# A 64-column copy moved from ScalarE to GpSimd in a fused attention and FFN kernel, with the order of all instructions planned anew

## The chip, the cores and the metric

The kernel runs on one core of one Trainium2 chip. The metric is the device time of one execution in microseconds (us), the median of several runs. The engines are TensorE (PE: matmul; PEld: its weight load), VectorE (DVE), ScalarE (ACT), GpSimd (POOL) and SyncE (SP), which here issues every DMA.

## The reference

What is computed, cut to what matters (8 batches, 8 heads, 576 positions, head size 64; 4608 tokens of width 512, FFN width 2048; all float32):

```python
scores = scale * np.matmul(q, k.transpose(0, 1, 3, 2))
thresh = np.max(scores, axis=-1, keepdims=True) - tau
scores = np.where(scores >= thresh, scores, -1000000000.0)
scores = scores - np.max(scores, axis=-1, keepdims=True)
attn = np.exp(scores)
attn = attn / (np.sum(attn, axis=-1, keepdims=True) + 1e-09)
x = np.matmul(attn, v)          # heads side by side: 4608 x 512
...
h = x @ w_in
r = np.maximum(h, 0.0)
return (s * (r * r) + b) @ w_out
```

## The kernel before, in words

**Pieces.** Float32 products are made of float16 pieces: a number is scaled, its high piece is its float16 value, its low piece the float16 value of the rest, and a product of two numbers is high x high + high x low + low x high. The helper `product` (line 327) writes the two 64-column halves of such a matmul side by side, so nearly all matmuls have line 327. Only batch 0 is computed in float32 (`plain_tile`, 36 tiles, at the start, while the weights are loaded and split).

**Tiles of attention.** Batches 1 to 7 are 252 split tiles (`split_tile`, line 621), each 128 queries of one head (or the last 64 of two heads) by 576 keys. A tile runs through all engines:

- TensorE makes the scores in bank s or t (line 643, 641).
- VectorE takes the row's maximum (line 646). GpSimd makes the threshold out of it (line 648, one column), ScalarE the bias (line 650) and the exponentials (line 652).
- VectorE drops what is below the threshold and sums the row (line 654). GpSimd adds the small constant (line 657, one column), VectorE takes the reciprocal (line 659).
- ScalarE writes the high pieces, `pieces[:, 0:S]` with S = 576 (line 660). Line 662 copies their first T = 64 columns to the columns S to S + T; ScalarE does it. VectorE writes the low pieces to the columns from S + T on (line 663).
- SyncE transposes `pieces[:, T:2S + T]`, that is high pieces 64 to 575, the copied 64, then the low pieces, into ea or eb (line 668). It waits for lines 660, 662 and 663. The buffer `en` is one of three.
- When a pair of heads has its tiles, TensorE multiplies ea and eb by the values (`with_v`, line 678), and ScalarE takes the result out of bank pv (line 685).

**The FFN.** When a block of 256 tokens is there, it runs in 16 steps of 128 FFN columns: TensorE makes h (24 matmuls), ScalarE takes the relu out of PSUM (line 902), squares it (905) and rounds it to the high piece (906), GpSimd makes the low piece (line 907, 128x256; VectorE in the last block), and TensorE multiplies by the second weights into bank o. Attention tiles of the next batches run among the steps of the earlier blocks.

**What sets the order.** The order of all instructions on each engine is made by a planner (`Plan`) before the kernel is emitted. Each operation is added with an engine, two costs in ns (how long it occupies the engine, and when its result is there), what it reads and writes, and a due time in tiles. `act`, `pool`, `dve` and `dve2` (lines 366 to 376) add for one engine; `dve2` and `pool` mark the operation as a user of one shared port, of which the planner lets only one run at a time. The planner places the operations by their due times forwards and backwards, then corrects single due times by the list `NUDGES` (from line 26), and places once more:

```python
for kind, n, many, by in NUDGES:
    for k in kinds[kind][n:n + many]:
        first[k] += by
```

A kind is all operations with the same engine and first cost, numbered as they first appear; an entry moves the due time of `many` of them, from the n-th on, by `by` ns. Kind 56 is the copy of line 662, 252 operations. Kinds 62 and 67 are TensorE's first and second products of the FFN, kind 45 small loads, kind 58 the transposes. Each engine runs its instructions strictly in the planned order; waits are on semaphores of the others.

Of the kernel before, what the change touches and what calls it, by code (L numbers as in the profile page):

```python
# [243 lines left out]
def tile_attention_ffn(ctx: ExitStack, tc: tile.TileContext, qT, kT, v, tau, w_in, w_out, s, b, out):  # L244


    nc = tc.nc
    P = 128
    B, H, D, S = qT.shape
# [3 lines left out]
    T = S - M  # L253
# [118 lines left out]
    def act(cost, fn, r, w, at):  # L372
        plan.add("ACT", cost, fn, r, w, at)
# [800 lines left out]
```

## Time and profile before

| | |
|---|---|
| runs | 1104.88, 1105.57, 1108.40 us; median 1105.57 us |
| the profiled execution | 1103.84 us, of which the span (first to last instruction) is 1102.0 us |
| granted TensorE clock | 1.00 of full speed (2.4 GHz), in the mean and in every slice |
| instructions | 38579 |
| DMA | 157.05 MB moved, mean 143 GB/s |

The profile was taken of one execution. Its rows give, for an engine or a group of instructions, the busy time, the mean of one, and the idle time of the engine just ahead of it with what ended that idle time (its releaser). The spans of matmuls have modelled ends, and spans on GpSimd are rough. Idle time of an engine that is not the bottleneck costs nothing by itself.

### The profile page before, as it was taken

The page shows a single profiled execution, that of the slowest core. Times are in us where ns is not written, and L with a number is a line of the kernel's source. Part 1 is how long each engine was busy: PE and PEld are TensorE (multiplying, and loading weights), DVE is VectorE, ACT ScalarE, POOL GpSimd, SP SyncE. Part 2 cuts the span into 40 slices and gives each one's busy share as a digit, 9 for nine tenths or more (in the row PEclk, how much of TensorE's full clock was granted, in tenths as well). Part 3 has the DMA queues.
Part 4 walks back from the last instruction along what each step waited for, and adds up shares of the span by engine and source line. Part 5 has one row for each costly group of instructions (what it writes and reads, how often), then busy time and mean ns, then how long its engine had stood idle before and what let it go on. Part 6 is the DMA issues. An engine that isn't in the chain of part 4 may idle for free.

```text
span 1102.0 us, 38579 instructions
## 1 busy us (share of the span) xinstructions
PE 1085.7 (99%) x15122; PEld 934.5 (85%) x15122; DVE 916.0 (83%) x1948; ACT 964.3 (88%) x2293; POOL 543.9 (49%) x1115
## 2 busy tenths in 40 slices
PE   8999999999999999999999999999999999999998
PEld 7767778899888888988888889988888888888888
DVE  6899999999999899989898999979989887984022
ACT  7998989999999989998989898989989998996443
POOL 6546555555545555545554455535445554542300
PEclk9999999999999999999999999999999999999999
DMA  9940269789988899888787888879797776583000
GB/s 275 362 160 2 68 151 197 125 168 183 189 140 157 143 199 152 166 132 172 161 136 124 155 165 162 139 118 185 153 176 122 156 134 142 95 126 61 7 21 21
DMA packets 359222, 157.05 MB, mean 143 GB/s; under 512 B 313344, under 2 KB 340736, under 8 KB 359040
## 3 DMA queue, kind: packets, MB, share of 16 engines
q1 hardware_dynamic: 359040, 154.60, 71.3%
q8 instruction: 118, 1.93, 0.8%
q14 instruction: 64, 0.52, 0.2%
HBM read 46.01 MB, written 9.44 MB: 50 GB/s over the span
## 4 chain that ended last, share of the span: by engine, by line
PE 69%; ACT 12%; DVE 8%; DMA 6%; issue 4%; SPq 1%; POOL 1%; ACTq 0%; DVEq 0%; POOLq 0%
PE o L327 24%; PE h L327 23%; PE pv L678 7%; PE s L327 5%; PE t L327 5%; DMA eb<-en 3%; ACT en L660 3%; ACT em L652 2%; DMA ea<-en 2%; DVE em L654 2%; ACT iw L902 1%; DVE en L663 1%; DVE st L646 1%; PE t L601 1%; PE pv L614 1%
## 5 line engine op out<-in xcount | busy, mean ns | idle before, releaser
L327 PEld LDWEIGHTS <-iw 128*64 128x64 f16 x6912 | 392.9, 110 | 28.6 <-issue 5.7
L327 PE MATMUL h<-xp,iw 128*64 128x256 f16 x6456 | 406.4, 273 | 2.2 <-ACT iw L902 1.6
L327 PEld LDWEIGHTS <-gs 128*64 128x64 f16 x3552 | 242.0, 110 | 74.4 <-issue 0.2
L907 POOL TENSOR_TENSOR gs<-iw,gs 128x256 f16<-128x256 f32 x272 | 197.6, 727 | 191.9 <-ACT gs L906 77.7
L327 PE MATMUL o<-ow,gs 128*64 128x512 f16 x1890 | 242.6, 379 | 0.0
L663 DVE SCALAR_TENSOR_TENSOR en<-em,st,en 128x576 f16<-128x576 f32 x252 | 208.7, 831 | 23.6 <-ACT en L660 21.6
L660 ACT ACTIVATE en<-em,st 128x576 f16<-128x576 f32 x252 | 193.5, 770 | 14.8 <-DVE st L659 6.0
L327 PE MATMUL o<-iw,gs 128*64 128x512 f16 x1470 | 191.6, 379 | 0.0
L648 POOL TENSOR_SCALAR st<-st,wz 128x1 f32<-128x1 f32 x252 | 125.3, 498 | 109.9 <-DVE st L646 75.8
L657 POOL TENSOR_SCALAR st<-st 128x1 f32<-128x1 f32 x252 | 89.5, 355 | 135.9 <-DVE em L654 87.2
L902 ACT ACTIVATE iw<-h 128x256 f32<-128x256 f32 x269 | 101.6, 378 | 43.8 <-PE h L327 38.0
L905 ACT ACTIVATE iw<-iw 128x256 f32<-128x256 f32 x288 | 119.5, 416 | 3.4
L906 ACT CAST gs<-iw 128x256 f16<-128x256 f32 x288 | 115.6, 403 | 4.9 <-PE o L327 0.7
L327 PEld LDWEIGHTS <-ow 128*64 128x64 f16 x1568 | 101.6, 110 | 13.3 <-issue 0.5
L654 DVE SCALAR_TENSOR_TENSOR em<-t,st,em 128x576 f32<-128x576 f32 x126 | 102.2, 811 | 12.3 <-ACT em L652 6.3
L654 DVE SCALAR_TENSOR_TENSOR em<-s,st,em 128x576 f32<-128x576 f32 x126 | 102.1, 810 | 8.4 <-ACT em L652 5.5
L652 ACT ACTIVATE em<-t,st,wz 128x576 f32<-128x576 f32 x126 | 104.1, 827 | 2.3 <-DVE en L663 1.4
L652 ACT ACTIVATE em<-s,st,wz 128x576 f32<-128x576 f32 x126 | 104.1, 826 | 1.0
L646 DVE TENSOR_REDUCE st<-s 128x1 f32<-128x576 f32 x126 | 94.5, 750 | 11.7 <-PE s L327 10.8
L646 DVE TENSOR_REDUCE st<-t 128x1 f32<-128x576 f32 x126 | 94.5, 750 | 9.7 <-PE t L327 8.7
L650 ACT ACTIVATE st<-st,wz 128x1 f32<-128x1 f32 x252 | 73.1, 290 | 19.5 <-DVE st L646 18.6
L678 PE MATMUL pv<-eb,ow 128*64 128x256 f16 (+1 forms) x588 | 78.9, 286 | 0.9 <-DMA eb<-en 0.9
(198 smaller groups left out, 1649.8 us busy)
## 6 DMA issues: line engine op xcount, KB each, us to landing
ow<-k SPq DMA_DIRECT2D x98, 216.0 KB, 3.9
rk<-in_k_dram SPq DMA_DIRECT2D x29, 288.0 KB, 3.8
iw<-in_moe_w_in_dram SPq DMA_DIRECT2D x16, 512.0 KB, 9.5
ow<-in_moe_w_out_dram SPq DMA_DIRECT2D x16, 512.0 KB, 9.6
rq<-in_q_dram SPq DMA_DIRECT2D x28, 288.0 KB, 3.8
out_dram<-iw SPq DMA_DIRECT2D x31, 256.0 KB, 3.0
rv<-in_v_dram SPq DMA_DIRECT2D x56, 128.0 KB, 3.2
qs<-k SPq DMA_DIRECT2D x14, 216.0 KB, 3.4
```

The source lines that it names most:

```text
L327: nc.tensor.matmul(out[own], stat[:, own], moving, start=start, stop=stop)
L646: dve((667, 750), lambda: nc.vector.tensor_reduce(out=top, in_=ps, axis=mybir.AxisListType.XY, op=ALU.max, negate=True), [bk], [(ks_, 0)], ...
L648: pool((290, 255), lambda: nc.gpsimd.tensor_scalar(out=line, in0=top, scalar1=-1.0, scalar2=va.wz[:, 2:3], op0=ALU.mult, op1=ALU.add), [(k ...
L652: act((716, 885), lambda: nc.scalar.activation(out=halves, in_=ps, func=AF.Exp, bias=bias, scale=va.wz[:, 1:2]), [bk, (ks_, 4), (va.kwz, 1 ...
L654: dve((738, 820), lambda: nc.vector.scalar_tensor_tensor(out=halves, in0=ps, scalar=line, in1=halves, op0=ALU.is_ge, op1=ALU.mult, accum_o ...
L660: act((666, 760), lambda: nc.scalar.activation(out=pieces[:, 0:S], in_=ex, func=AF.Copy, scale=unit), [em_k, (ks_, 3)], [en_k], i)
L663: dve2((728, 830), lambda: nc.vector.scalar_tensor_tensor(out=pieces[:, S + T:2 * S + T], in0=ex, scalar=unit, in1=pieces[:, 0:S], op0=ALU ...
L678: nc.tensor.matmul(ps[j * D:(j + 1) * D], hd.values()[:, (n + 1) % 5, u * D:(u + 1) * D], lazy[("ea", "eb")[j]][:, n, g.c0:g.c0 + g.n], st ...
L902: act((264, 400), lambda: nc.scalar.activation(out=g(), in_=ps, func=AF.Relu, scale=H_DOWN), [h, (f"w{SPARES[(0, 1, 5)[k3]]}", "i", 2)], [ ...
L905: act((307, 430), lambda: nc.scalar.activation(out=g(), in_=g(), func=AF.Square), [kg], [kg], at)
L906: act((295, 405), lambda: nc.scalar.copy(out=hi, in_=g()), [kg], [f"gh{k3}"], at)
L907: do((735, 735) if not self.last else (400, 490), lambda: eng.tensor_tensor(out=lo, in0=g(), in1=hi, op=ALU.subtract), [kg, f"gh{k3}"], [f ...
```

## The change

Line 662 becomes an instruction of GpSimd, with other costs for the planner (occupied 260 ns, result after 250 ns, where ScalarE had 135 and 225), and with GpSimd's mark as a user of the shared port. It reads and writes the same columns and has the same place in the program; what waits for it is the same. In `NUDGES` the 34 entries of kind 56, which belonged to the old copy, are taken out; 321 entries are appended, over 57 kinds, among them 7 for kind 56, which is now GpSimd's copy, 39 for kind 67, 22 for kind 45, 20 for kind 62 and 17 for kind 58. The list goes from 655 entries to 942. Nothing else is changed. The diff, with most of the list cut:

```diff
 NUDGES = (
...
-    (73, 2, 6, -4809), (23, 7, 17, -916), (62, 5, 5, 3875), (25, 17, 19, -13768), (49, 34, 22, 1138), (29, 2, 2, -2426), (56, 148, 6, -6574), (74, 6, 2, -4235),
+    (73, 2, 6, -4809), (23, 7, 17, -916), (62, 5, 5, 3875), (25, 17, 19, -13768), (49, 34, 22, 1138), (29, 2, 2, -2426), (74, 6, 2, -4235), (21, 166, 10, 12067),
...
+    (67, 514, 46, 349), (22, 208, 1, 2624), (62, 52, 3, -1385), (53, 243, 9, 901), (43, 3, 3, 8544), (11, 7, 4, 907), (38, 44, 5, 5396), (13, 31, 1, 4746),
+    (69, 13, 2, -1317), (72, 3, 3, -2323), (45, 69, 5, -924), (55, 196, 4, 7572), (50, 78, 15, -6298), (68, 11, 1, -949),
 )
...
         act((666, 760), lambda: nc.scalar.activation(out=pieces[:, 0:S], in_=ex, func=AF.Copy, scale=unit),
             [em_k, (ks_, 3)], [en_k], i)
-        act((135, 225), lambda: nc.scalar.copy(out=pieces[:, S:S + T], in_=pieces[:, 0:T]), [en_k], [(en_k, 1)], i)
+        pool((260, 250), lambda: nc.gpsimd.tensor_copy(out=pieces[:, S:S + T], in_=pieces[:, 0:T]), [en_k], [(en_k, 1)], i)
         dve2((728, 830), lambda: nc.vector.scalar_tensor_tensor(
             out=pieces[:, S + T:2 * S + T], in0=ex, scalar=unit, in1=pieces[:, 0:S], op0=ALU.mult, op1=ALU.subtract),
             [em_k, en_k, (ks_, 3)], [(en_k, 2)], i)
```

## Rows read from the trace of the kernel before

**Rows 1.** The page, busy time, share and instructions of each engine.

```profile
PE 1085.7 (99%) x15122; PEld 934.5 (85%) x15122; DVE 916.0 (83%) x1948; ACT 964.3 (88%) x2293; POOL 543.9 (49%) x1115
```

**Rows 2.** Windows: stretch, length, then busy us (instructions) of each engine, clock, DMA.

```profile
100.00:200.00 100.00, 99.43 (x1377) 79.03 (x1373) 92.75 (x182) 93.22 (x214) 54.49 (x95) 1.00 0.60 124
200.00:300.00 100.00, 99.06 (x1436) 88.34 (x1433) 95.63 (x209) 95.50 (x239) 56.72 (x115) 1.00 0.89 167
300.00:400.00 100.00, 98.99 (x1437) 85.85 (x1434) 90.83 (x199) 92.54 (x228) 53.64 (x109) 1.00 0.87 155
400.00:500.00 100.00, 98.75 (x1442) 88.59 (x1438) 92.72 (x197) 92.83 (x232) 48.90 (x104) 1.00 0.91 159
500.00:600.00 100.00, 99.45 (x1431) 86.23 (x1427) 88.28 (x192) 89.65 (x218) 53.47 (x108) 1.00 0.78 151
600.00:700.00 100.00, 98.46 (x1434) 89.04 (x1431) 91.56 (x189) 90.31 (x222) 50.72 (x102) 1.00 0.82 157
700.00:800.00 100.00, 99.70 (x1439) 86.61 (x1436) 89.08 (x188) 91.19 (x225) 48.23 (x105) 1.00 0.82 147
800.00:900.00 100.00, 99.90 (x1445) 86.71 (x1441) 88.01 (x186) 93.24 (x224) 51.67 (x104) 1.00 0.79 145
900.00:1000.00 100.00, 100.00 (x1454) 86.98 (x1452) 83.10 (x178) 91.35 (x227) 48.08 (x102) 1.00 0.71 125
sum 900.00, PE 893.73 PEld 777.38 DVE 811.97 ACT 829.84 POOL 465.93; mean PE 99.30 PEld 86.38 DVE 90.22 ACT 92.20 POOL 51.77
```

**Rows 3.** Waits of TensorE from 100 us on: us in total, times, longest.

```profile
PE pv L678 <- DMA eb<-en: 2.2, 3, 1.3
PE h L327 <- ACT iw L902: 1.6, 6, 0.4
PE pv L327 <- ACT x L685: 0.6, 2, 0.4
PE s L327 <- DVE em L654: 0.5, 1, 0.5
PE pv L327 <- ACT xt L685: 0.5, 1, 0.5
```

**Rows 4.** Timeline, TensorE, at 581.94 us: start, us, engine, instruction, idle before.

```profile
581.94 1.28 PE L327 MATMUL h<-xp,iw 128*64 128x256 f16 x20 [0.44 <-ACT iw L902]
```

**Rows 5.** Groups of instructions by line: busy us, mean ns, then idle before.

```profile
L662 ACT COPY en<-en 128x64 f16<-128x64 f16 x252 | 59.3, 238 | 0.9
L663 DVE SCALAR_TENSOR_TENSOR en<-em,st,en 128x576 f16<-128x576 f32 x252 | 208.7, 831 | 23.6 <-ACT en L660 21.6
L648 POOL TENSOR_SCALAR st<-st,wz 128x1 f32<-128x1 f32 x252 | 125.3, 498 | 109.9 <-DVE st L646 75.8 <-DVE st L659 19.3 <-ACT gs L906 3.0
L657 POOL TENSOR_SCALAR st<-st 128x1 f32<-128x1 f32 x252 | 89.5, 355 | 135.9 <-DVE em L654 87.2 <-DVE st L659 13.1 <-ACT iw L902 5.0
L451 POOL TENSOR_SCALAR qs<-qs,bound 128x576 f32<-128x576 f32 x2 | 1.5, 743 | 2.2 <-ACT em L585 2.2
```

**Rows 6.** Single lines: ns min/median/max, first and last start; landing of line 668's transposes.

```profile
L657 POOL TENSOR_SCALAR st<-st x252: 192/192/1158, 136.9 to 995.0; 128x1 f32<-128x1 f32 x126
...
L648 POOL TENSOR_SCALAR st<-st,wz x252: 257/268/1464, 130.5 to 991.1; 128x1 f32<-128x1 f32 x126
...
L663 DVE SCALAR_TENSOR_TENSOR en<-em,st,en x252: 792/814/1307, 144.5 to 998.0; 128x576 f16<-128x576 f32 x126
...
DMA to landing us min/median/max: 2.8/3.7/6.7
```

**Rows 7.** Timeline, VectorE and GpSimd, 600.60 to 601.46 us, inside one tile.

```profile
600.60 0.82 DVE L663 SCALAR_TENSOR_TENSOR en<-em,st,en 128x576 f16<-128x576 f32 x1
...
600.77 0.69 POOL L657 TENSOR_SCALAR st<-st 128x1 f32<-128x1 f32 x1 [0.92 <-ACT iw L902]
```

**Rows 8.** Waits of SyncE's queue: us in total, times, longest.

```profile
SPq L668 <- DVE en L663: 144.0, 101, 5.5
...
SPq L668 <- ACT en L662: 44.7, 32, 2.6
```

188 rows, old and new, of the table NUDGES are left out of this document.

## The prediction

> **What bounds the kernel now.** First the busy table: TensorE is busy 1085.7 of 1102.0 us, ScalarE 964.3, VectorE 916.0, GpSimd 543.9 [rows 1]. Only 16.3 us of the span have no matmul in them, so the kernel is bound by TensorE, and its matmuls are not touched. The change can give back no more than the time that TensorE waits. Where is that time? The stretches of 100 us show it [rows 2]: from 100 to 1000 us TensorE is busy 893.73 of 900 us, idle 6.27; the low pieces of all 252 split tiles run between 144 and 999 us [rows 6], so the change works inside this stretch. The other 10.1 us (16.3 less 6.27) lie before 100 us, where loads and plain tiles set the pace, and at the very end, where the last output block leaves.
>
> A busy TensorE is not one at its peak, because ends of matmuls are modelled, so I look for hidden waits in the same rows by counting matmuls: 1454 in the stretch from 900 to 1000 us, which has no idle time, against 1431 to 1445 in the seven others from 200 on. Summing 1454 less each count over the seven stretches from 200 to 900 us gives 18+17+12+23+20+15+9 = 114 matmuls, and at 14.54 matmuls per us that is 7.8 us. The mix of sizes differs a little and some records may be missing, so 7.8 us is an estimate. It and the 6.27 us say the same: six to eight microseconds is what the split stage could give back.
>
> Who ends these waits? In TensorE's list of waits from 100 us on [rows 3], 2.7 us of the 5.4 us shown end with ScalarE (1.6 after the relu of the FFN's first product, 0.6 and 0.5 after evacuations of the values), 2.2 us with transposes that land in eb, 0.5 us with VectorE. So half of TensorE's waits are on ScalarE, which is busy 92.2% of that stage; VectorE is next with 90.2%, GpSimd has 51.8% [rows 2]. One such wait stands in the timeline at 581.94 us: the matmuls of h wait 0.44 us for a relu [rows 4].
>
> **The change, part by part.**
>
> The copy leaves ScalarE: 252 instructions of 238 ns on average, 59.3 us in all, go [rows 5]. ScalarE's share in the split stage falls from 829.84 of 900 us to about 770.5, 85.6%. That is not time off the span. It shortens ScalarE's queue by 0.24 us in each tile, and the relu or evacuation behind it comes that much earlier.
>
> The copy comes to GpSimd: no copy of 128x64 f16 is in the trace. From below, a one-column operation (line 657) takes 192 ns at least [rows 6]; from above, a 576-column one of f32 (line 451) takes 743 ns [rows 5]. On the line between them 64 columns cost 192 + 63/575 x 551 = 252 ns. I take 0.25 us because 64 columns are much nearer to one.
>
> It does not run beside VectorE's low pieces in the good sense. The timeline shows it [rows 7]: the low pieces (line 663) run from 600.60 to 601.42 us, and a one-column operation of GpSimd that began at 600.77 took 0.69 us instead of 0.19, ending at 601.46, just behind them. The Trainium skill, in Perfetto Trace Analysis, section Optimizing Scalar/DVE Operations, says that GpSimd and VectorE share an SBUF read port and that moving work between those two might not help; this trace agrees with 0.69 us against 0.19 us.
>
> Line 663 and the copy are released by the same instruction, line 660, so many copies will meet this. Lines 648 and 657 show how much it costs on average over all cases: means of 498 and 355 ns [rows 5] against medians of 268 and 192 [rows 6], so some 160 to 230 ns. The copy, tied to line 660, should meet it rather oftener; I take 0.25 us. That makes 0.50 us each and 252 x 0.50 = 126 us; GpSimd goes from 543.9 to about 670 us, 61%. The ends are 0.25 us (all copies run clear, 607 us) and 0.95 us, a whole line 663 (0.81 us at the median [rows 6]) and some 0.14 us behind it (783 us, 71%). GpSimd is not the bound at either end. What is behind the copy in its queue are lines 648 and 657 of neighbouring tiles and line 907 of the FFN. A tile comes every 900/252 = 3.6 us, of which GpSimd now works 465.93/252 = 1.85 us; with the copy 2.1 to 2.8 us, so the cover is 0.8 us a tile even at the bad end. I cost its share of the path at nothing, with the bad case as a rival.
>
> The transposes come later: each waits for the copy and for line 663. Before, the copy took 0.24 us at once behind line 660 and was mostly done before line 663 (0.81 us). Now a blocked copy ends some 0.1 to 0.3 us behind line 663. The queue's waits show both releasers, 144.0 us in 101 transposes for line 663 and 44.7 us in 32 for the old copy, which at times stood behind other work on ScalarE [rows 8]; those 32 gain. A transpose takes 2.8 to 6.7 us to land [rows 6], so 0.2 us more is small against it, but TensorE's three waits for eb grow by 3 x 0.2 = 0.6 us. Bounds: a gain of the same size if the 32 late copies were those that matter, a loss of twice that.
>
> VectorE's line 663 may in turn start while a copy runs. From below this costs nothing. From above, all 252 could be delayed by a whole copy, 252 x 0.25 = 63 us on an engine with 88 us idle in the stage [rows 2]. I take it near nothing, since the mean of 831 ns against a median of 814 [rows 5, 6] contains what today's GpSimd operations do to it.
>
> The order planned anew: 34 corrections of the old copy's planned times go and 321 are appended, over 57 kinds of instruction, so every queue changes (SyncE's and GpSimd's too). The trace of before cannot show the new order. I bound it by its stretches [rows 2]: if all nine from 100 us on were like the best (no idle, 1454 matmuls), 7.8 us would go; if all were like the worst (600 to 700, 1.54 us idle), 9 x 1.54 - 6.27 = 7.6 us would come. Between them I take a gain of 1 us, a little to the good side of the middle: the three stretches from 700 us on have 0.3 us of idle time or less each, so that orders with hardly a wait exist for this mix of work, and the relieved ScalarE makes them easier to have.
>
> **The sum.** ScalarE ends half of TensorE's waits (2.7 of 5.4), and half of 7.8 us is 3.9 us; with a shorter queue I count all of it as gone. Plus 1 us for the order, minus 0.6 us for the transposes: 4.3 us gained. The profiled execution took 1103.84 us (span 1102.0 and 1.8 around it), so it would take 1099.5. The median of the runs, 1105.57, is 1.7 us above the profiled one; from it the forecast is 1101.3, and I give **1101.2 us**. About 0.3%, 3.3 us, is what a measurement of this kernel can tell from no change; the forecast lies only just beyond that.
>
> **Rivals.**
>
> A, the forecast: ScalarE's relief reaches TensorE. Own range 1098 to 1102.2 us. For it: half of TensorE's waits end with ScalarE [rows 3]. Against it: TensorE is at 99.3% of the stage already. Chance 0.37.
>
> B, nothing to be seen: VectorE, at 90.2% against ScalarE's 92.2% [rows 2], is loaded as much, sits in the same chain of each tile, and gets nothing off. Then the waits on ScalarE turn into waits on VectorE or on transposes, and the gain is 0 to 3 us: 1102.5 to 1106, most likely 1104.5. For it: VectorE was at 95.6% from 200 to 300 us, above ScalarE's 95.5%. Against it: VectorE itself ends 0.5 us of TensorE's waits only [rows 3]. Chance 0.37.
>
> C, slower, by one mechanism: blocked copies hold GpSimd's queue. The copy waits in order for line 660 and then for the port until line 663 is done, up to 0.95 us; line 648 or 657 of the next tile stands behind it, then VectorE's line 654 or 659 waits, and then ScalarE's line 660. It decides from the point where a copy's hold exceeds the 0.8 us a tile of cover, that is, where nearly all copies are at the bad end or are planned before their line 660 is done. Its price: all nine stretches like the worst, 7.6 us, plus the transposes' 0.6 us, so up to 1113.8; a part of it, say half, gives 1109.7. For it: the 0.69 us of the one-column operation [rows 7]. Against it: GpSimd is idle almost half of the stage [rows 2]. Chance 0.18.
>
> D, the new order takes away nearly all of the stage's waits: 7.8 us, 1097.8, or a few more if the start's part of the 10.1 us shrinks as well, since the corrections reach the plain tiles too; down to 1095. Chance 0.08.
>
> That the change does not do what it says is half true already: where the copy runs behind the low pieces and not beside them, it costs what C and the sum say, no more.
>
> **How the numbers follow.** Faster by over 0.3% (below 1102.3): A and D, 0.45. Within 0.3%: B, 0.37. Slower: C, 0.18. The range from 1096 to 1109 leaves out the lower end of D and the upper half of C.
>
> **What would show it.** ScalarE's busy time about 905 us. GpSimd's copies at 0.25 us clear of line 663 and 0.6 to 0.95 us inside it, its busy time 610 to 780 us. TensorE's idle time from 100 to 1000 us below 4 us, with fewer waits on line 902 and on the evacuations, and over 1440 matmuls in most stretches: right for A. The same 6 us of idle time under other names: B. Waits of VectorE for lines 648 and 657 above today's, more idle time of TensorE, and the copy named as releaser of the transposes: C. The prediction is wrong if the time moved before 100 us or after 1000 us, which I leave as they are, or if the copy costs much over 0.3 us where nothing blocks it.

## The result, and the profile after

The changed kernel takes **1114.01 us** (median of 5 runs, 1111.58 to 1115.98) against 1106.36 us of the kernel before (5 runs beside it, 1104.88 to 1108.40): ratio **1.0073, 95% interval [1.0051, 1.0094]**. It is slower by some 8 us, where the forecast was 1101.2 us in a range from 1096 to 1109. The profiled execution took 1113.26 us, its span 1111.5 us.

In the profile after, lines below the list `NUDGES` stand 36 further down: 327 is now 363, 509 is 545, 654 is 690, 660 is 696, 662 is 698 (the copy), 663 is 699, 668 is 704, 678 is 714, 902 is 938. First the page's busy times, to be read beside [rows 1].

```profile
PE 1088.0 (98%) x15122; PEld 931.6 (84%) x15122; DVE 916.5 (82%) x1948; ACT 938.3 (84%) x2041; POOL 617.0 (56%) x1367
```

252 instructions left ScalarE and came to GpSimd, as the diff says. TensorE's idle time went from 16.3 to 23.5 us (1111.5 less 1088.0), and its busy time from 1085.7 to 1088.0 us. The windows of the kernel after, in the form of [rows 2], say where:

```profile
200.00:300.00 100.00, 94.22 (x1319) 81.21 (x1317) 89.30 (x191) 85.30 (x188) 58.79 (x132) 0.98 0.92 162
300.00:400.00 100.00, 97.85 (x1419) 86.11 (x1416) 92.51 (x198) 89.58 (x200) 61.45 (x137) 1.00 0.83 150
400.00:500.00 100.00, 99.88 (x1444) 86.95 (x1439) 94.29 (x201) 89.13 (x198) 62.89 (x141) 1.00 0.85 150
...
sum 900.00, PE 886.26 PEld 765.79 DVE 806.55 ACT 794.83 POOL 535.89; mean PE 98.47 PEld 85.09 DVE 89.62 ACT 88.31 POOL 59.54
```

From 100 to 1000 us TensorE is idle 900 less 886.26, 13.7 us, where it was 6.3 us [rows 2]; and 7.9 us of it lie between 200 and 400 us (100 less 94.22, and 100 less 97.85), against 2.0 before. The stretch from 200 to 300 us has 1319 matmuls for 1436, and a granted clock of 0.98: it is there that the work fell behind. Windows inside it:

```profile
278.00:282.00 4.00, 1.78 (x21) 1.16 (x19) 1.87 (x3) 0.89 (x2) 2.01 (x3) 0.94 1.17 176
281.00:285.00 4.00, 3.41 (x34) 2.88 (x36) 0.18 (x2) 0.00 (x0) 0.00 (x0) 0.57 1.08 266
...
282.00:284.00 2.00, 2.00 (x24) 1.66 (x20) 0.00 (x0) 0.00 (x0) 0.00 (x0) 0.50 1.04 221
```

From 281 to 285 us ScalarE and GpSimd do nothing and VectorE 0.18 us, all at once. TensorE works, but 34 matmuls in 4 us, at a granted clock of 0.57 in the mean, and from 282 to 284 us of 0.50, the lower of its two levels (1.2 GHz). Before the clock fell it had been idle: the window in front, which reaches one microsecond into the next, has it busy 1.78 us of 4, and the timeline shows a wait of 2.07 us that ended at 281.59. The timeline of these microseconds, lines chosen:

```profile
276.56 1.56 SPq L704 DMA_TRANSPOSE eb<-en  x1
...
279.21 0.17 PE L363 MATMUL pv<-vm,onesb 128*64 128x4 bf16 x1
...
281.59 0.42 PE L714 MATMUL pv<-eb,vt 128*64 128x256 f16 x1 [2.07 <-DMA eb<-en]
...
284.36 0.42 PE L714 MATMUL pv<-eb,vt 128*64 128x256 f16 x1
...
284.82 0.16 DVE L545 TENSOR_SCALAR vs<-pv 128x3 f32<-128x3 f32 x1 [4.95 <-PE pv L714]
...
285.83 0.77 ACT L696 ACTIVATE en<-em,st 128x576 f16<-128x576 f32 x1 [6.94 <-DVE st L695]
...
285.94 0.20 POOL L553 TENSOR_TENSOR vs<-vs,spread 128x3 f32<-128x3 f32 x1 [5.09 <-DVE vs L547]
```

Read it from the bottom. ScalarE's high pieces (line 696) waited 6.94 us for VectorE's reciprocal, and GpSimd 5.09 us for VectorE. VectorE itself stood at line 545 for 4.95 us, until the group of values products (line 714) was done. Line 545 has nothing to do with that group: it reads the maxima of the next batch's inputs, which TensorE had written at 279.21 with one small product. But these maxima lie in bank pv, columns 420 and up, and the group writes columns 0 to 255 of the same bank. In the program as built, VectorE's wait is for the last matmul of the group that is emitted in between. The Trainium skill, in PSUM — Partial Sum Buffer, section PSUM bank collisions raise a hardware error, says to guard PSUM with semaphores by bank and quadrant, not by address; the 4.95 us wait agrees, for the columns differ and the bank is the same. The group, in turn, came late: the transpose of its pieces had been issued at 276.56, and TensorE waited 2.07 us for it.

The planner cannot know of this. It keeps the maxima and the values under different keys:

```python
ktop = ("top", 420 + 4 * n)
pe(1, 64, lambda: product(top, onesb, vm[m]), ks + ["onesb"], [ktop], at)
dve((72, 155), lambda: nc.vector.tensor_scalar(
    out=x[:, 0:3], in0=top[:, 0:3], scalar1=SMALLEST, scalar2=None, op0=ALU.max), [ktop], [kx], at)
...
plan.add("PE", (cost, cost + 180), products, g.keys + [k for hd in g.hds for k in hd.kvs], ["pv"], at, True)
```

Some of VectorE's and TensorE's waits in the kernel after show how often it happens, and what stands in place of [rows 3]:

```profile
DVE vs L545 <- PE pv L714: 10.7, 4, 5.0
...
DVE power L839 <- PE pv L714: 0.9, 1, 0.9
...
DVE st L695 <- POOL st L693: 9.0, 24, 1.2
```

```profile
PE pv L714 <- DMA eb<-en: 5.0, 4, 2.1
PE h L363 <- ACT iw L938: 3.5, 6, 1.0
...
PE t L677 <- DVE em L690: 1.9, 2, 1.1
...
PE o L363 <- DVE iw L971: 1.5, 1, 1.5
```

Five such reads (10.7 + 0.9 = 11.6 us) stand behind a group of values in the new order, two in the order before (0.8 us shown, in one wait). And TensorE waits 5.0 us for eb instead of 2.2, 3.5 us for relus instead of 1.6.

The copy itself, by its group and by its single line:

```profile
L698 POOL COPY en<-en 128x64 f16<-128x64 f16 x252 | 88.1, 351 | 84.4 <-ACT en L696 59.8 <-POOL st L693 5.5 <-issue 5.4
```

```profile
L698 POOL COPY en<-en x252: 229/238/1191, 139.2 to 1007.0; 128x64 f16<-128x64 f16 x126
```

It takes 238 ns at the median and 351 in the mean, cheaper than forecast, and GpSimd's 617 us are far from a bound. So is it the copy, or the order?

### The profile page after: what moved, and what is told of

Same layout as the page of the kernel before. It is cut to its first block, busy times and chain, and to the rows that moved or that the text cites. A ratio compares the mean times of both kernels' runs of the same rounds, so it can differ in the third digit from the quotient of the medians.

```text
span 1111.5 us, 38795 instructions
## 1 busy us (share of the span) xinstructions
PE 1088.0 (98%) x15122; PEld 931.6 (84%) x15122; DVE 916.5 (82%) x1948; ACT 938.3 (84%) x2041; POOL 617.0 (56%) x1367
## 4 chain that ended last, share of the span: by engine, by line
PE 64%; ACT 5%; DMA 5%; DVE 3%; issue 2%; POOL 0%; SPq 0%; ACTq 0%; DVEq 0%; POOLq 0%
PE o L363 24%; PE h L363 23%; PE pv L714 7%; PE s L363 5%; PE t L363 4%; DMA ea<-en 2%; DMA eb<-en 2%; ACT en L696 1%; ACT em L688 1%; DVE en L699 1%; ACT iw L938 1%; PE t L677 1%; PE pv L363 0%; PE s L677 0%; ACT k L558 0%
## 5 line engine op out<-in xcount | busy, mean ns | idle before, releaser
L363 PE MATMUL o<-ow,gs 128*64 128x512 f16 x1890 | 239.7, 379 | 0.0
L699 DVE SCALAR_TENSOR_TENSOR en<-em,st,en 128x576 f16<-128x576 f32 x252 | 212.8, 848 | 19.7 <-ACT en L696 18.0
L693 POOL TENSOR_SCALAR st<-st 128x1 f32<-128x1 f32 x252 | 84.1, 334 | 92.7 <-DVE em L690 48.9
L698 POOL COPY en<-en 128x64 f16<-128x64 f16 x252 | 88.1, 351 | 84.4 <-ACT en L696 59.8
```

The source lines that it names most:

```text
L363: nc.tensor.matmul(out[own], stat[:, own], moving, start=start, stop=stop)
L698: pool((260, 250), lambda: nc.gpsimd.tensor_copy(out=pieces[:, S:S + T], in_=pieces[:, 0:T]), [en_k], [(en_k, 1)], i)
L699: dve2((728, 830), lambda: nc.vector.scalar_tensor_tensor(out=pieces[:, S + T:2 * S + T], in0=ex, scalar=unit, in1=pieces[:, 0:S], op0=ALU ...
```

## The experiments

All were timed in five rounds beside the kernel before, and every ratio is to the runs of the kernel before on the same chip. A planned order depends on the engine and costs that an operation is added with; which engine then executes it can be set apart from that.

**The copy against the order.** Two kernels split the change. e1 has the order of the changed kernel, but executes the copy on ScalarE; e2 has the order of before, and executes the copy on GpSimd:

```diff
-        pool((260, 250), lambda: nc.gpsimd.tensor_copy(out=pieces[:, S:S + T], in_=pieces[:, 0:T]), [en_k], [(en_k, 1)], i)
+        pool((260, 250), lambda: nc.scalar.copy(out=pieces[:, S:S + T], in_=pieces[:, 0:T]), [en_k], [(en_k, 1)], i)
```

> The order of every queue is that of the changed kernel, but the copy in its place is emitted for ScalarE. Theory 1 (the copy on GpSimd costs the time: it waits for the low pieces and holds GpSimd's queue and the transposes): the time falls back to about 1106 us, ratio to the kernel before 1.000 to 1.002. Theory 2 (the newly planned order costs it, whichever engine copies): stays slow, 1112 to 1117 us, ratio 1.005 to 1.010; ScalarE is back at about 964 us busy.

Measured: 1117.76 us, ratio 1.0120 [1.0102, 1.0139], beyond even what was expected of a costly order. The edit of e2, in the kernel before:

```diff
-        act((135, 225), lambda: nc.scalar.copy(out=pieces[:, S:S + T], in_=pieces[:, 0:T]), [en_k], [(en_k, 1)], i)
+        act((135, 225), lambda: nc.gpsimd.tensor_copy(out=pieces[:, S:S + T], in_=pieces[:, 0:T]), [en_k], [(en_k, 1)], i)
```

> The order of every queue is that of the kernel before, only the copy is emitted for GpSimd at the place where it stood among all instructions. Theory 1: slow like the changed kernel, 1111 to 1117 us, ratio 1.005 to 1.010 or more, since the order does not know of the port. Theory 2: like the kernel before or a little faster, 1103 to 1107 us, ratio 0.997 to 1.001.

Measured: 1103.63 us, ratio 0.9996 [0.9983, 1.0008]. The busy times of its page, and then the group of its copies:

```profile
PE 1086.1 (99%) x15122; PEld 924.8 (84%) x15122; DVE 917.7 (83%) x1948; ACT 939.9 (85%) x2041; POOL 610.5 (55%) x1367
```

```profile
L662 POOL COPY en<-en 128x64 f16<-128x64 f16 x252 | 86.8, 345 | 84.0 <-ACT en L660 66.4 <-issue 5.0 <-POOL st L657 3.5
```

The same 252 copies on GpSimd, at the same 345 ns, in the old order: neither gain nor loss. The new order, with the copies left on ScalarE: over 1% slower. **The order made the kernel slower, not the copy.** In the new order the copy is even better off on GpSimd, 1.0073 against 1.0120; that order was planned for it there.

**What the corrections do.** e3 is the changed kernel without the 321 new corrections of due times, that is with the list of before less the entries of the copy. e4 is the kernel before, the copy on ScalarE, without its own 34 entries for the copy.

One of the lines that e4 changes (the others in the same way):

```diff
-    (19, 9, 4, 9071), (45, 21, 3, -5118), (20, 221, 12, -3551), (52, 48, 8, -6492), (17, 58, 34, 836), (56, 44, 36, 722), (65, 239, 49, 2398), (69, 25, 3, 2895),
+    (19, 9, 4, 9071), (45, 21, 3, -5118), (20, 221, 12, -3551), (52, 48, 8, -6492), (17, 58, 34, 836), (65, 239, 49, 2398), (69, 25, 3, 2895),
```

> GpSimd's copy with its costs in the plan, but without the 321 appended corrections (the 621 old ones that are left stay). If the corrections that were appended spoil a good order, this is faster than the changed kernel, under 1111 us. If they repaired what the new place of the copy broke, it is slower, 1118 us or more.

Measured: 1126.44 us, ratio 1.0195 [1.0176, 1.0215].

> The kernel before with its 34 corrections of kind 56 taken out and nothing else: a control for what any new planning does. Theory 2 in its general form (any order that is not the one of before costs 5 us or more): 1110 to 1116 us. If small changes of the order do little: 1104 to 1108 us.

Measured: 1117.18 us, ratio 1.0116 [1.0097, 1.0134], somewhat beyond what was expected. So an order loses 1.2% when nothing but 34 corrections of one cheap operation are dropped. Of the four orders measured here, that of before is the best, and the 321 corrections repaired some of what the change of engine and the 34 dropped entries had upset, 1.95% to 0.73%.

**The read of the bank.** e5 takes the wait at line 545 away: VectorE reads a constant in SBUF there instead of the bank. The scales of the batches then come from ones and not from the data. e6 does the same to the kernel before (line 509).

```diff
-                out=x[:, 0:3], in0=top[:, 0:3], scalar1=SMALLEST, scalar2=None, op0=ALU.max), [ktop], [kx], at)
+                out=x[:, 0:3], in0=ones.bitcast(F32)[:, 0:3], scalar1=SMALLEST, scalar2=None, op0=ALU.max), [ktop], [kx], at)
```

> The changed kernel, its order untouched, but VectorE's first step on a batch's tops (line 545) reads a tile of ones in SBUF and not the tops in bank pv, so that it waits neither for TensorE's small product nor for a group of values that was emitted between the two (scales then come from ones and not from the data). Theory 3 (the new order puts five groups of values between the small product and this read, VectorE is held up to 5 us and ScalarE and GpSimd with it): 4 to 7 us faster than the changed kernel, ratio to the kernel before 1.000 to 1.004; the 5 us hole of VectorE near 280 us is gone. Rival (the late transposes alone hold TensorE, the bank read only rides on them): ratio stays 1.006 or more.

Measured: 1108.02 us, ratio 1.0034 [1.0021, 1.0047].

> The same edit on the kernel before, the control. Its trace shows two such holds of under 1 us each. Both theories: ratio 0.998 to 1.001.

Measured: 1103.46 us, ratio 0.9988 [0.9976, 1.0001].

e7 keeps the whole computation, and emits the read ahead of the group of values products where the planner had put it behind (5 places). e8 does the same to the kernel before (2 places). In the edit, r is VectorE's read and m the small product that it reads; it works on the order that the planner has made. The lines that collect reads and groups are left out here.

```diff
...
+        for r, m in self.reads:
+            where = {n: k for k, n in enumerate(order)}
+            between = [g for g in self.groups if where[m] < where[g] < where[r]]
+            if between and all(where[d] < min(where[g] for g in between) for d in ops[r][4]):
+                order.remove(r)
+                order.insert(order.index(min(between, key=where.get)), r)
...
```

> The changed kernel with its computation whole, but where a group of values stood between the small product and VectorE's read of it, the read is emitted ahead of the group (5 places; all other operations keep their order). Theory 3: like the run without the bank read, ratio 1.000 to 1.004, perhaps a little more, since TensorE's group now waits for the read. Rival: 1.006 or more.

Measured: 1107.45 us, ratio 1.0027 [1.0011, 1.0042].

> The same move in the kernel before (2 places). Both theories: ratio 0.998 to 1.001; a gain of up to 1 us under theory 3.

Measured: 1104.01 us, ratio 0.9990 [0.9979, 1.0001]. Five instructions in other places, nothing else: the changed kernel goes from 1.0073 to 1.0027. Two edits of different kinds, e5 and e7, take away the same 0.4 to 0.5%. TensorE's waits in e7, from 100 us on:

```profile
PE pv L722 <- DMA eb<-en: 3.3, 3, 1.4
...
PE pv L722 <- DVE vs L552: 1.3, 4, 0.5
```

(Line 722 is 714 of the changed kernel, 552 is 545.) Now the groups wait for the reads ahead of them, although the two touch different columns: the program's dependency is one of the whole bank.

**Does it hold in other orders?** The same move in e2 (e9, 2 places), e3 (e10, 7 places), e1 (e11, 5 places) and e4 (e12, 3 places).

> The order of before, the copies on GpSimd, and VectorE's reads of the batches' tops emitted ahead of the values groups (2 places). The copy cost nothing in this order (0.9996) and the two reads of before were worth 0.1% (0.9990). Theory 3: 0.998 to 1.000, about 1103 us; no part of the change but its order costs time. Against it: the relieved ScalarE pays once the holds are gone, then under 0.997.

Measured: 1104.52 us, ratio 1.0010 [0.9999, 1.0020], at the upper end of what was expected and no better than e2. No version that computes everything beats the kernel before by more than can be told.

> The GpSimd copy with the corrections of before only (1.0195), reads emitted ahead of the values groups in 7 places. VectorE's holds on that bank in its profile sum to 6.0 us. Theory 3: the gain is about that, 0.4 to 0.6%, so 1.013 to 1.016; the larger part of that order's loss lies elsewhere. Rival: a hold is covered by other work, nothing changes, 1.018 to 1.021.

Measured: 1122.52 us, ratio 1.0171 [1.0152, 1.0190], between the two expectations: 0.24% for 6.0 us of waits.

> The order of the changed kernel with the copies on ScalarE (1.0120), reads moved in 5 places. VectorE's holds in its profile sum to some 9.8 us. Theory 3: about the same gain as with the copies on GpSimd (0.0073 to 0.0027), so 1.007 to 1.008. Rival: the holds matter only beside the GpSimd copies, 1.011 to 1.013.

Measured: 1113.14 us, ratio 1.0084 [1.0066, 1.0103], just beyond what was expected, with an interval that holds it.

> The kernel before without its 34 corrections of the copy (1.0116), reads moved in 3 places. VectorE's hold on that bank in its profile is 1.8 us only. Theory 3: the gain follows the holds, 0.1 to 0.2%, so 1.009 to 1.011; a fresh order then loses about 1% by something else. Rival: the move helps by 0.4% whatever the holds, 1.007 to 1.008.

Measured: 1113.82 us, ratio 1.0097 [1.0081, 1.0113]. The move helps by 0.46% in the changed kernel and by 0.36% in its order with the copies on ScalarE (e11). In the two other orders the steps of 0.24 and 0.19% (e10, e12) are within the intervals, and in the order of before the move brings 0.1% (e8) or nothing (e9). It is not worth the sum of the waits: a wait of VectorE is in part covered. So what makes it expensive at 281 us?

**The late transpose.** In e13 to e15 the values products multiply the values themselves in place of the transposed pieces. The matmuls and transposes are the same in number and size, but none waits for the other. These kernels leave out the weighting of the values by attention.

```diff
-                                     lazy[("ea", "eb")[j]][:, n, g.c0:g.c0 + g.n], start=(i == 0), stop=(i == len(slots) - 1))
+                                     hd.values().rearrange("p t d -> p (t d)")[:, 0:g.n], start=(i == 0), stop=(i == len(slots) - 1))
```

> The changed kernel with its reads moved, and the values products multiply the values themselves in place of the transposed pieces: same matmuls and same transposes, but TensorE no longer waits for a transpose, nor a transpose for TensorE (the output is then not the attention of the data). With the waits it was 1.0027. If the 0.3% that was left is late transposes (3.3 us of TensorE's waits, DMA at 0.92 to 1.15 of its share where they fall), it falls by 0.3%: 0.999 to 1.001, and TensorE's idle time from 200 to 400 us falls from 7.7 to under 4.5 us. If the rest is the relus and VectorE (4.3 us there), it stays at 1.001 to 1.004.

Measured: 1105.86 us, ratio 1.0020 [1.0007, 1.0033], inside what was expected if the rest lies with the relus and VectorE.

> The same edit on the kernel before with its reads moved (0.9990). TensorE waited 1.9 us for transposes there: 0.997 to 0.999. The difference of the two is what the order still costs once transposes are out of it.

Measured: 1102.63 us, ratio 0.9984 [0.9971, 0.9997].

> The same edit on the changed kernel itself (1.0073): the reads stay behind the values groups, but no group waits for a transpose. If the holds cost by themselves, some 0.4% of it stays: 1.003 to 1.005. If a hold only hurts where the group in front of it is late by its transpose (as at 279 us, 2.07 us), it falls to 1.000 to 1.002, like the kernel with its reads moved and no waits.

Measured: 1106.74 us, ratio **1.0024 [1.0013, 1.0034]**, between the two expectations. Here the reads stand where the changed kernel has them. Waits of VectorE and TensorE in e15, and its timeline at the place of the 4.95 us:

```profile
DVE vs L545 <- PE pv L714: 7.3, 4, 3.2
...
PE t L677 <- DVE em L690: 2.3, 2, 1.2
PE o L363 <- DVE iw L971: 1.5, 1, 1.5
```

```profile
279.81 1.70 PE L714 MATMUL pv<-vt 128*64 128x256 f16 x28
...
281.56 0.16 DVE L545 TENSOR_SCALAR vs<-pv 128x3 f32<-128x3 f32 x1 [1.55 <-PE pv L714]
```

At 281 us the group no longer waits, and its 28 matmuls take 1.70 us at a granted clock of 1.00, where in the changed kernel they ran from 281.59 on at the lower clock; the hold falls from 4.95 to 1.55 us. The kernel is as fast as with the reads moved (1.0027), and both edits together bring no more (1.0020): the two gains do not add up.

The traces do not make them one event, though. In e15 the other holds stay as they were. In the changed kernel VectorE is held for 3.15 us up to 743.64 and for 1.86 us up to 870.34, behind groups that TensorE did not wait for; TensorE then waits for VectorE. The changed kernel, then e15:

```profile
748.68 1.49 PE L363 MATMUL o<-iw,gs 128*64 128x512 f16 x12 [1.49 <-DVE iw L971]
...
872.75 0.68 PE L677 MATMUL t<-ow 128*64 128x288 f16 x8 [1.14 <-DVE em L690]
```

```profile
743.74 1.49 PE L363 MATMUL o<-iw,gs 128*64 128x512 f16 x12 [1.48 <-DVE iw L971]
...
868.22 0.68 PE L677 MATMUL t<-ow 128*64 128x288 f16 x8 [1.14 <-DVE em L690]
```

In e7 both waits are gone, but the late transpose is not:

```profile
200.00:300.00 100.00, 94.66 (x1360) 82.56 (x1356) 92.10 (x196) 87.58 (x194) 60.48 (x136) 1.00 0.92 163
300.00:400.00 100.00, 97.61 (x1407) 85.22 (x1404) 92.31 (x198) 88.56 (x197) 61.34 (x137) 1.00 0.84 151
```

```profile
282.94 0.30 PE L722 MATMUL pv<-eb,vt 128*64 128x256 f16 x1 [1.40 <-DMA eb<-en]
```

From 200 to 400 us TensorE idles as long in e7 (7.7 us) as in the changed kernel (7.9 us). What e7 saves in its trace is above all the stretch at the slow clock (the clock was 1.00 here) and the waits behind the later holds. The lower clock does not follow from the wait either. In e1, where the same group waited as long for its transpose, the clock stayed at 1.00 and VectorE was held 3.45 us, not 4.95:

```profile
284.25 0.30 PE L714 MATMUL pv<-eb,vt 128*64 128x256 f16 x1 [2.05 <-DMA eb<-en]
...
284.00:286.00 2.00, 1.75 (x32) 1.75 (x34) 0.00 (x0) 0.00 (x0) 0.00 (x0) 1.00 1.06 227
...
286.00 0.16 DVE L545 TENSOR_SCALAR vs<-pv 128x3 f32<-128x3 f32 x1 [3.45 <-PE pv L714]
```

So the reads are shown to cost 0.4 to 0.5% of the changed kernel, and so are the waits between groups and transposes, but why the two do not add up, and how the 5 us divide among holds, late transpose and clock, stays open. The edit of e15 also frees the transposes from waiting for TensorE; that part is not told apart.

What is left is e13 against e14, 0.36%, some 4 us. Windows of e13, then of e14:

```profile
200.00:300.00 100.00, 98.00 (x1421) 85.14 (x1418) 93.22 (x199) 89.09 (x197) 61.38 (x138) 1.00 0.89 165
300.00:400.00 100.00, 97.13 (x1390) 83.50 (x1388) 93.40 (x203) 89.76 (x201) 62.65 (x143) 1.00 0.86 154
```

```profile
200.00:300.00 100.00, 99.51 (x1448) 86.33 (x1444) 95.82 (x211) 95.95 (x240) 57.11 (x115) 1.00 0.92 168
300.00:400.00 100.00, 99.46 (x1446) 86.32 (x1444) 91.64 (x200) 93.40 (x230) 54.02 (x110) 1.00 0.87 156
```

TensorE idles 4.9 us there in e13 and 1.0 in e14. TensorE's waits of e13 from 200 to 400 us name VectorE and the relu:

```profile
PE t L370 <- DVE em L698: 1.8, 1, 1.8
PE h L370 <- ACT iw L948: 1.7, 2, 1.1
PE t L685 <- DVE em L698: 1.1, 1, 1.1
```

(Line 370 is 363 of the changed kernel, 698 is 690, 948 is 938.) After 400 us e13 has some 2.7 us less idle time than e14, and the spans of these two executions are only 0.8 us apart (1103.1 and 1102.3 us), since e13's is its fastest of 11. So the two traces do not explain the difference of 4 us; which instructions of the new order bring it about stays open.

## Why the prediction was wrong

**What bounds it** was right. TensorE is the bound, and the 9.5 us by which the span grew are its idle time in the split stage for the greater part (7.5 us). Another 2.3 us are longer busy time; the matmuls at the lower clock from 281.59 account for some 1.5 us of it (3.2 us for what took 1.70 in e15).

**The step that failed** is the last term, "Between them I take a gain of 1 us" for the order planned anew. The order cost some 8.5 us (1.0073 less 0.9996, of 1104), at the bad end of that step, 7.6 us, or beyond; with the copies left on ScalarE it cost 13 us (e1). Two reasons given there were wrong. "Orders with hardly a wait exist for this mix of work" is no ground to expect one: the two orders made without the corrections of the copy lost 1.2 and 2.0% (e4, e3), and the 321 corrections brought the second to 0.7%. And averages of 100 us do not show what an order can do: more than half of the loss (0.0046 of 0.0073, 5 us) went with five reads of 0.16 us each, placed behind groups in the same bank. Where the other 3 us come from is open. The bounds of the step were worked out, but the range took in less than half of the bad one: 1109 us is 3.4 us above 1105.57.

**ScalarE's relief**, 3.9 us, failed too, in two ways. The old order with the copies gone from ScalarE gains nothing (e2, 0.9996), although ScalarE ended half of TensorE's waits. That is rival B's time, and in part its reason. In e2's trace TensorE idles 4.7 us from 100 to 1000 us, not 6.3: its waits for relus fall from 1.6 to 1.1 us, those for VectorE rise from 0.5 to 1.0 us, and before 100 us, where the copy does not run, 1.0 us of idle time is added. And the relief is smaller than 252 x 238 ns = 59.3 us [rows 5]: ScalarE's busy time fell by 24.4 us in e2 (964.3 less 939.9), 97 ns a copy, so that about 905 us was wrong. The timeline of the kernel before shows how:

```profile
600.32 0.37 ACT L902 ACTIVATE iw<-h 128x256 f32<-128x256 f32 x1
600.58 0.24 ACT L662 COPY en<-en 128x64 f16<-128x64 f16 x1
600.72 0.42 ACT L905 ACTIVATE iw<-iw 128x256 f32<-128x256 f32 x1
```

Neighbours overlap on both sides: the relu ends at 600.69, the copy lasts from 600.58 to 600.82, the square starts at 600.72. Here 0.14 us lie between the copy's start and the next one, and its record lasts 0.24 us. In the new order the move is worth 0.5% (e1 against the result; e11 against e7 0.6%), but the relus do not show why: TensorE waits 3.6 us for them in e1 and 3.5 us in the changed kernel. That order was planned without the copy on ScalarE.

**The copy's price** was close. Forecast 0.25 us clear of line 663, measured 0.238; forecast 0.50 in the mean, measured 0.351, inside the bounds. GpSimd came to 617 instead of 670 us. "0.6 to 0.95 us inside" line 663 is what the timeline of the kernel after shows:

```profile
267.95 0.82 DVE L699 SCALAR_TENSOR_TENSOR en<-em,st,en 128x576 f16<-128x576 f32 x1
268.04 0.83 POOL L698 COPY en<-en 128x64 f16<-128x64 f16 x1 [1.30 <-issue]
```

It ends 0.10 us behind line 699. But half of all copies took 238 ns or less, so that fewer met it than I took. The Trainium skill, in SBUF — State Buffer, section Terms, says that the two engines arbitrate for a shared port pair, which is held for the full instruction while the other one blocks; the 0.83 us agree.

**The transposes** were to add 0.6 us to TensorE's waits for eb, which grew by 2.8 us (2.2 to 5.0) in the changed kernel. In e2 they fell to 1.3 us, so that the price of the later copy is nothing and the growth is the order's.

**VectorE's line 663** (848 ns for 831, 212.8 us for 208.7) cost 4 us of an engine with idle time, as taken.

**Rival C** gave the sign and nearly the size (up to 1113.8 us), with a chance of 0.18, but not by its mechanism. Blocked copies in GpSimd's queue would have cost time in e2, which has the same copies, and without them the new order is slower still (e1). The sign named for C is there in both: transposes wait for the copy 53.5 us in SyncE's queue in the changed kernel and 57.8 us in e2, where nothing was lost. VectorE's waits for line 693 did grow, from 5.0 to 9.0 us, but not in e2 (4.9 us).

## What to carry to other kernels

When a change replans the order of everything, cost the order first and by itself: emit the old work in the new order, and the new work in the old. A planner must know a PSUM bank as one resource for readers and writers alike, or it can put a short read behind a long group of matmuls; what that costs has to be measured, for it was less than the sum of the waits here. Two edits that each bring 0.5% and together no more need not mend the same wait: compare their traces place by place. On an engine whose records overlap, an instruction's duration is more than its removal gives back.

## What the runs showed of the hardware

- VectorE's read of 3 columns of a PSUM bank waited 4.95 us for matmuls into other columns of it, and with the read moved ahead (e7) the matmuls waited for the read. The wait is the program's, made for the whole bank; what the chip would do without it was not tried.
- After TensorE had waited 2.07 us, its granted clock was 0.50 from 282 to 284 us in the kernel after, and pairs of 256-column matmuls followed each other every 0.21 us. After a wait of 2.05 us for the same group in e1 the clock was 1.00, and the pairs came every 0.11 us. So such a wait can be paid for twice, but need not be.
- ScalarE's records overlap: 252 copies of 238 ns each, gone, freed 24.4 us of its busy time and not 59.3.
